# Attention and two feed-forward stages: whole q and k loads, two pairs by units, another list

## The chip, the cores and the metric

One of the eight cores of a Trainium2 chip runs the kernel. The metric is the device time of one execution in microseconds, lower being better. Before the change three runs gave 909.26, 910.92 and 911.55 us, a median of 910.92.

## What is computed

q, k and v are (4, 8, 576, 64) in f32. Attention is local: each chunk of 64 positions attends to itself alone. Its output goes through two feed-forward stages whose weights arrive as f64.

```python
scores = scale * np.matmul(q_c, k_c.transpose(0, 1, 2, 4, 3))   # per 64-position chunk
scores = scores - np.max(scores, axis=-1, keepdims=True)
attn = np.exp(scores)
attn = attn / (np.sum(attn, axis=-1, keepdims=True) + 1e-09)
x = np.matmul(attn, v_c)           # then (B*S, H*D) = (2304, 512)
y = ((x @ w_a) * (x @ w_b)) @ w_out                    # 512 -> 1536 -> 512
h = y @ w_in                                           # 512 -> 2048
out = (np.maximum(h, 0) + alpha * np.minimum(h, 0)) @ w_out2    # -> 512
```

## The kernel before

**Tiling.** The 2304 tokens are 18 units of 128 (two chunks of 64). Two units are a pair (U = 2), nine pairs in all, and attention works on a pair at a time. For the feed-forward stages units are gathered in five blocks: block 0 has two units (256 columns), blocks 1 to 4 have four (512 columns). Each f32 product is made of three f32r matmuls, of a high and a low half of either factor, so every activation and every weight is split in two.

**The list.** All of attention and the first feed-forward group are written out in START (L30 to L41) as tokens; `perform` (L504) runs them one by one. Every engine works off its own tokens strictly in that order, and waits for the data of each. A number is that of the unit, pair or weight block, or block and part.

- Lk, Lw: load q and k, and v, of a unit (sync queue, three buffers each; a load waits until the unit three before is read). `load` (L367) makes three DMAs of each: the even heads of all 128 partitions, and twice 64 partitions of the odd heads, with the halves exchanged.
- s: scores of a pair (TensorE, 64 matmuls of 64x64, L393); m, u: maximum and subtraction (VectorE, L401, L409); e: exponential (ScalarE, L417); z, r: sum and reciprocal (VectorE, L421 to L427); n: normalise (GpSimd, L431); t: four transposes of a unit (TensorE, L440); c: their copy to SBUF (ScalarE, L445); v: products with v of a pair (TensorE, 64 matmuls, L461); h, l: high half (ScalarE, L475) and low half (VectorE, L479) of x. The tiles s and px share two PSUM buffers of two banks.
- Lf: fetch of a weight block, 512 KB of f64 (sync queue, two buffers, L93). o: two passes on ScalarE (L103, L104); d: three on VectorE (L111 to L115); a: an addition on GpSimd (L125); H: high half (ScalarE, L130); W: low half (VectorE, L135). Blocks 0 to 3 are two of w_a and two of w_b, 4 and 5 are of w_out, 6 and 7 belong to the next group.
- F j.q: first products of block j, 12 matmuls (q = 0, 2 with w_a; 1, 3 with w_b); E: their way out (ScalarE copy, or VectorE product L262); h j.q, g j.q: high half (ScalarE) and low half (GpSimd, L238) of the product. B, D: second product (6 matmuls) and its way out.

F j needs h and l of all pairs in block j: F0 those of pair 0, F1 of pairs 1 and 2, F2 of 3 and 4, F3 of 5 and 6. F j.0 needs weight block 0, j.1 block 1, j.2 block 2, j.3 block 3; B needs blocks 4 and 5.

**After the list** (L531) come the first products of block 4, which read x of pairs 7 and 8, and then the groups of both stages, block by block, with one weight conversion (`job`) every fifth step. That code isn't changed.

Of the kernel before, what the change touches and what calls it, by code (L numbers as in the profile page):

```python
# [44 lines left out]
def tile_attention_moe_moe2(ctx: ExitStack, tc: tile.TileContext, qkv, w_a, w_b, w_out, w2_in, alpha, w2_out, out):  # L45
# [92 lines left out]
    WA = {}
# [46 lines left out]
        halved[0] += 1  # L185
        block_at[b] = half_high(block_at[b], jobs[b][0], jobs[b][2])

    def w_halves(b):
        m, dst, tag = jobs[b][:3]
        dst[m] = half_low(*block_at.pop(b), m, tag)  # L190

    def job(limit):

        b = halved[0]
        if b < begun[0] and jobs[b][0] < limit:
            w_high(b)
# [163 lines left out]
    with tc.manual_schedule():  # L360
# [58 lines left out]
        def at_sum(p):  # L419
            sm = ap.tile([P, U * HP, 2, 1], F32, tag="sm", name="sm")  # L420
            nc.vector.tensor_reduce(out=sm.rearrange("p h i o -> p h (i o)"), in_=prob[p], op=ALU.add, axis=AX.X)  # L421
            rec_of[p] = sm
# [6 lines left out]
        def at_norm(p):  # L429
            e = prob[p]  # L430
            nc.gpsimd.tensor_tensor(  # L431
                out=e, in0=e, in1=rec_of.pop(p).to_broadcast([P, U * HP, 2, 64]), op=ALU.mult
            )
# [14 lines left out]
        def at_pv(p):

            px = pss.tile([P, 2, HP // 2, U * P], F32, tag="s", name="px")  # L450
            for k in range(U):
                pt = pt_of.pop(U * p + k)
                t = v_t.pop(U * p + k)
                for h2 in range(HP // 2):
# [11 lines left out]
            px_of[p] = px.rearrange("p o h n -> p h o n")

        def x_part(x, c):
            return x.rearrange("p (h o) n -> p h o n", o=2)[:, :, :, c:c + U * P]

        def at_xh(p):
# [1 line left out]
            if c == 0:
                new_x(b)
            nc.scalar.activation(out=x_part(xh[b], c), in_=px_of[p], func=ACTF.Copy)  # L475

        def at_xl(p):
            b, c = block_of[p]
            nc.vector.tensor_tensor(  # L479
                out=x_part(xl[b], c), in0=px_of.pop(p), in1=x_part(xh[b], c).bitcast(F32), op=ALU.subtract  # L480
            )
# [111 lines left out]
```

## Time and profile before

| | |
|---|---|
| span of the profiled execution | 909.1 us |
| its time | 911.02 us |
| median of three runs | 910.92 us |
| TensorE matmuls | 883.1 us busy, 97%, 5208 instructions |
| VectorE, ScalarE, GpSimd | 501.4, 287.2, 297.2 us busy |
| mean granted TensorE clock | 0.992 of full speed |
| DMA | 55.36 MB, mean 61 GB/s |
| chain that ended last | TensorE 93%, DMA 3%, sync queue 3% |

PE is TensorE's matmuls, PEld its weight loads, DVE is VectorE, ACT ScalarE, POOL GpSimd, SPq the sync engine's DMA queue. Matmuls overlap, so a row's duration is longer than the step to the next. PEclk is the clock granted to TensorE, 1.00 being 2.4 GHz and about 0.5 the lower level, 1.2 GHz. The chain of waits follows what released each piece of work back from the end. In brackets behind a row stands the idle time before it and what ended it.

### The profile page before, as it was taken

What the parts mean: (1) busy time and instruction counts of PE and PEld (TensorE: products, weight loads), DVE (VectorE), ACT (ScalarE), POOL (GpSimd) and SP (SyncE); (2) the same over time, 40 slices, a digit from 0 to 9 for tenths busy, and PEclk for the clock granted to TensorE, in tenths of its full rate; (3) what the DMA queues carried; (4) which work ended last, traced back from release to release, by engine and by line L of the source; (5) the groups of instructions that cost most, each with busy time, mean ns of one, the idle gap of its engine ahead of it and who ended that gap; (6) DMA issues with size and microseconds to landing.
All of it is one profiled execution on the core that took longest, in us unless ns stands there. A gap on an engine that the chain in (4) does not pass through costs nothing.

```text
span 909.1 us, 12839 instructions
## 1 busy us (share of the span) xinstructions
PE 883.1 (97%) x5208; PEld 742.6 (82%) x5208; DVE 501.4 (55%) x772; ACT 287.2 (32%) x499; POOL 297.2 (33%) x243
## 2 busy tenths in 40 slices
PE   4789999999999999999999999999999999999998
PEld 3678888888888888888888888888888888888886
DVE  3678543443454444444353453777767676768554
ACT  2456445331422332232243353312222231223010
POOL 1333333321322222232155632333333233324131
PEclk9899999999999999999999999999999999999999
DMA  8795412210110111011010011111102010200013
GB/s 195 180 233 138 116 47 70 66 51 24 47 62 31 47 47 47 24 48 56 14 63 32 1 47 47 46 47 34 59 26 69 24 47 24 70 24 23 1 70 139
DMA packets 59242, 55.36 MB, mean 61 GB/s; under 512 B 5168, under 2 KB 53296, under 8 KB 59184
## 3 DMA queue, kind: packets, MB, share of 16 engines
q1 hardware_dynamic: 59184, 54.55, 20.8%
q8 instruction: 41, 0.67, 0.3%
q14 instruction: 17, 0.14, 0.0%
HBM read 49.82 MB, written 4.72 MB: 60 GB/s over the span
## 4 chain that ended last, share of the span: by engine, by line
PE 93%; DMA 3%; SPq 3%; ACT 1%; DVE 1%; issue 0%; ACTq 0%
PE po L228 38%; PE ph L228 22%; PE pb L228 15%; PE pa L228 15%; SPq L371 2%; DMA qk_t<-in_qkv 1%; DMA raw<-in_moe_w_out 1%; PE px L461 1%; SPq L368 1%; PE s L393 1%; PE pt L440 1%; SPq L93 0%; ACT t L103 0%; ACT wh L130 0%; DVE e L409 0%
## 5 line engine op out<-in xcount | busy, mean ns | idle before, releaser
L238 POOL TENSOR_TENSOR gl<-neg,gh 128x512 fp32r<-128x512 f32 (+1 forms) x80 | 94.8, 1185 | 184.7 <-ACT gh L233 179.8
L125 POOL TENSOR_TENSOR t<-t,raw 128x512 int32<-128x512 int32 x68 | 89.3, 1313 | 190.0 <-issue 87.9
L233 ACT ACTIVATE gh<-neg 128x512 fp32r<-128x512 f32 (+1 forms) x80 | 47.3, 591 | 278.3 <-DVE neg L322 270.3
L238 POOL TENSOR_TENSOR gl<-a_sb,gh 128x512 fp32r<-128x512 f32 (+1 forms) x60 | 71.2, 1186 | 184.9 <-ACT gh L233 179.4
L228 PE MATMUL ph<-xh,wh 128*128 128x512 f32 (+1 forms) x320 | 117.7, 368 | 0.0
L228 PE MATMUL ph<-xl,wh 128*128 128x512 f32 (+1 forms) x320 | 117.7, 368 | 0.0
L228 PE MATMUL ph<-xh,wl 128*128 128x512 f32 (+1 forms) x320 | 117.7, 368 | 0.0
L262 DVE TENSOR_TENSOR a_sb<-pb,a_sb 128x512 f32<-128x512 f32 (+1 forms) x60 | 38.1, 636 | 139.3 <-PE pb L228 138.5
L228 PE MATMUL po<-wh,gl 128*128 128x512 f32 x288 | 112.1, 389 | 0.0
L228 PE MATMUL po<-wl,gh 128*128 128x512 f32 x288 | 112.1, 389 | 0.0
L228 PE MATMUL po<-wh,gh 128*128 128x512 f32 x288 | 112.0, 389 | 0.0
L135 DVE TENSOR_TENSOR wl<-t,wh 128x512 fp32r<-128x512 f32 x68 | 69.8, 1028 | 72.9 <-ACT wh L130 72.9
L340 DVE TENSOR_TENSOR oacc<-po,oacc 128x512 f32<-128x512 f32 x126 | 83.5, 686 | 33.1 <-PE po L228 33.1
L319 DVE TENSOR_SCALAR neg<-ph,alpha_sb 128x512 f32<-128x512 f32 (+1 forms) x80 | 55.7, 696 | 73.5 <-PE ph L228 71.2
L228 PE MATMUL po<-gh,wl 128*128 128x512 f32 (+1 forms) x240 | 90.0, 375 | 3.2 <-DVE wl L135 3.2
L228 PE MATMUL pa<-xh,wl 128*128 128x512 f32 (+1 forms) x240 | 89.3, 372 | 2.1 <-ACT ptt_t L445 2.1
L228 PE MATMUL po<-gl,wh 128*128 128x512 f32 (+1 forms) x240 | 89.3, 372 | 0.0
L228 PE MATMUL po<-gh,wh 128*128 128x512 f32 (+1 forms) x240 | 89.2, 372 | 0.0
L228 PE MATMUL pa<-xl,wh 128*128 128x512 f32 (+1 forms) x240 | 88.9, 370 | 0.0
L228 PE MATMUL pa<-xh,wh 128*128 128x512 f32 (+1 forms) x240 | 88.9, 370 | 0.0
L228 PE MATMUL pb<-xh,wl 128*128 128x512 f32 (+1 forms) x240 | 88.7, 370 | 0.0
L228 PE MATMUL pb<-xl,wh 128*128 128x512 f32 (+1 forms) x240 | 88.3, 368 | 0.0
(53 smaller groups left out, 1498.3 us busy)
## 6 DMA issues: line engine op xcount, KB each, us to landing
raw<-in_moe_w_out SPq DMA_DIRECT2D x28, 512.0 KB, 3.5
raw<-in_moe_w_in SPq DMA_DIRECT2D x16, 512.0 KB, 3.7
raw<-in_moe_w_a SPq DMA_DIRECT2D x12, 512.0 KB, 3.7
raw<-in_moe_w_b SPq DMA_DIRECT2D x12, 512.0 KB, 3.6
qk_t<-in_qkv SPq DMA_DIRECT2D x18, 256.0 KB, 5.5
qk_t<-in_qkv SPq DMA_DIRECT2D x36, 128.0 KB, 5.1
out<-oacc SPq DMA_DIRECT2D x18, 256.0 KB, 2.0
v_t<-in_qkv SPq DMA_DIRECT2D x18, 128.0 KB, 3.7
```

The lines of the kernel that those rows point to most:

```text
L125: nc.gpsimd.tensor_tensor(out=ti, in0=ti, in1=raw[:, :, 0].bitcast(I32), op=ALU.add)
L135: nc.vector.tensor_tensor(out=wl, in0=wf, in1=wh.bitcast(F32), op=ALU.subtract)
L228: nc.tensor.matmul(out=dst, lhsT=a, rhs=b, start=(i == 0), stop=(i == len(steps) - 1))
L233: nc.scalar.activation(out=h, in_=src, func=ACTF.Copy)
L238: nc.gpsimd.tensor_tensor(out=l, in0=src, in1=h.bitcast(F32), op=ALU.subtract)
L262: nc.vector.tensor_tensor(out=a_sb, in0=G[m, j], in1=a_sb, op=ALU.mult)
L319: nc.vector.tensor_scalar(out=neg, in0=ph, scalar1=0.0, scalar2=alpha_sb[:, m:m + 1], op0=ALU.min, op1=ALU.mult)
L340: nc.vector.tensor_tensor(out=acc[j][:, t, :], in0=po, in1=acc[j][:, t, :], op=ALU.add)
L368: nc.sync.dma_start(out=t[:, 0::2, :], in_=src[:, 0::2, :])
L371: nc.sync.dma_start(out=t[64 * i:64 * i + 64, 1::2, :], in_=src[64 * o:64 * o + 64, 1::2, :])
L393: nc.tensor.matmul(out=s[q, i, k, hp, :], lhsT=t[r, 0, hp, q], rhs=t[r, 1, hp, q])
L440: nc.tensor.transpose(out=pt[:, hp, :], in_=e[:, h].rearrange("p i k -> p (i k)"), identity=ident)
```

## The change

`load_qk` fetches a unit's q and k with one DMA, in the order in which they lie in memory, and `load_v` fetches heads as two halves, the first whole and the second with exchanged partitions, in three DMAs as before. The exchange that q and k had in the load is made where the scores are written (`hp // 2 ^ i` in `at_scores`), and the indices of the transposes and of the products with v follow it; the tile e keeps the layout of the scores.

Every attention step takes an optional `k`: with it, it works on one unit of the pair, on one half of the same tiles (`part` makes a tile at its first use). Tokens ending in U ask for that: pairs 0 and 1 go unit by unit in s, m, u, e, z, r, n, v, h and l, the other pairs whole. Token V is W on GpSimd in place of VectorE; seven of the eight weight blocks of the list use V, the last one W. START is another order of the tokens, with the same matmuls in it.

```diff
-Lk0 Lk1 Lw0 Lw1 Lk2 s0 m0 Lk3 u0 Lf0 e0 Lw2 z0 s1 Lk4 r0 o0 m1 n0 Lk5 u1 t0 d0 e1 t1 c0 z1 a0 s2 c1 r1 H0 v0
-m2 n1 Lw3 h0 u2 Lw4 t3 l0 e2 t2 Lf1 c3 W0 c2 z2 F0.0 Lf2 r2 v1 E0.0 Lk6 n2 o1 h1 Lw5 d1 t4 o2 Lk7 t5 l1 a1
-c4 Lw6 c5 d2 H1 v2 Lf3 W1 s3 h2 Lk8 a2 l2 F0.1 H2 Lf4 m3 o3 F1.0 E0.1 Lk9 W2 h0.1 d3 F0.2 Lw7 o4 u3 g0.1 Lw8
...
+Lk0 Lf0 sU0 Lk1 mU0 uU0 o0 d0 Lk2 sU1 mU1 eU0 zU0 rU0 sU2 Lf1 o1 uU1 a0 nU0 Lk3 mU2 sU3 Lk4 d1 Lk5 a1 Lw0
+Lf2 uU2 Lw1 eU1 mU3 uU3 H0 eU3 zU1 t0 s2 V0 eU2 Lk6 Lk7 rU1 nU1 c0 o2 zU3 t1 c1 H1 vU0 zU2 rU2 Lw2 vU1 nU2
+hU0 rU3 m2 hU1 Lw3 t2 nU3 t3 c3 Lk8 c2 u2 lU0 s3 lU1 e2 F0.0 E0.0 vU2 V1 vU3 d2 z2 Lw4 a2 r2 H2 F0.1 Lf3 n2
+o3 m3 t5 hU2 u3 E0.1 V2 hU3 Lk9 Lw5 d3 Lk10 s4 lU2 lU3 a3 Lk11 Lw6 e3 t4 F0.2 Lk12 c5 c4 H3 m4 v2 u4 V3 F0.3
+Lf4 h0.1 g0.1 z3 h2 l2 e4 E0.2 s5 r3 z4 F1.0 r4 Lf5 n3 o4 E0.3 E1.0 Lk13 t6 m5 d4 F1.1 h0.3 Lk14 t7 n4 c6
+F1.2 E1.1 g0.3 o5 a4 u5 d5 a5 c7 e5 Lw7 t9 H4 z5 h1.1 g1.1 t8 v3 s6 H5 Lf6 F1.3 Lw8 h3 c9 r5 V4 E1.2 Lw9
+Lk15 m6 V5 n5 c8 l3 B0.0 Lw10 u6 v4 E1.3 t11 t10 s7 o6 D0.0 m7 h1.3 h4 c11 l4 g1.3 d6 e6 B0.1 z6 B1.0 B1.1
+c10 Lw11 a6 D0.1 D1.0 r6 Lf7 B0.2 o7 u7 v5 D0.2 h5 n6 D1.1 B1.2 Lw12 B0.3 d7 e7 Lk16 D0.3 B1.3 t12 D1.2 F2.2
+D1.3 z7 Lw13 r7 n7 t13 c12 l5 F2.0 F2.3 Lw14 c13 v6 E2.2 E2.3 E2.0 t15 F2.1 t14 h6 l6 E2.1 F3.0 Lw15 Lk17
+h2.3 h2.1 g2.3 c15 s8 Lw16 g2.1 B2.0 m8 H6 a7 c14 D2.0 E3.0 v7 F3.1 B2.1 E3.1 u8 F3.2 B2.2 h3.1 F3.3 h7 l7
+Lf8 e8 z8 H7 Lf9 D2.1 r8 E3.2 Lw17 n8 D2.2 E3.3 g3.1 V6 t17 t16 B2.3 c16 c17 v8 h8 h3.3 g3.3 l8 D2.3 W7
...
-    def half_low(wf, wh, m, tag):
+    def half_low(wf, wh, m, tag, eng):
         wl = wps[m % 4].tile([P, 512], F32R, tag=tag + "l", name="wl")
-        nc.vector.tensor_tensor(out=wl, in0=wf, in1=wh.bitcast(F32), op=ALU.subtract)
+        eng.tensor_tensor(out=wl, in0=wf, in1=wh.bitcast(F32), op=ALU.subtract)
...
-        def load(t, src):
-            nc.sync.dma_start(out=t[:, 0::2, :], in_=src[:, 0::2, :])
+        def load_qk(u):
+            t = ap.tile([P, 2, HP, P], F32, tag="qk", name="qk_t", bufs=3)
+            nc.sync.dma_start(out=t.rearrange("p a h n -> p (a h n)"), in_=qkv[u, :, 0:2 * HP * P])
+            qk_t[u] = t
+
+        def load_v(u):
+            t = ap.tile([P, HP, P], F32, tag="v", name="v_t", bufs=3)
+            src = qkv[u, :, 2 * HP * P:].rearrange("p (h n) -> p h n", n=P)
+            nc.sync.dma_start(out=t[:, 0:2, :], in_=src[:, 0:2, :])
             for i in range(2):
                 o = 1 - i
-                nc.sync.dma_start(out=t[64 * i:64 * i + 64, 1::2, :], in_=src[64 * o:64 * o + 64, 1::2, :])
-
-        def load_qk(u):
-            t = ap.tile([P, 2, HP, P], F32, tag="qk", name="qk_t", bufs=3)
-            load(t.rearrange("p a h n -> p (a h) n"), qkv[u, :, 0:2 * HP * P].rearrange("p (h n) -> p h n", n=P))
-            qk_t[u] = t
-
-        def load_v(u):
-            t = ap.tile([P, HP, P], F32, tag="v", name="v_t", bufs=3)
-            load(t, qkv[u, :, 2 * HP * P:].rearrange("p (h n) -> p h n", n=P))
+                nc.sync.dma_start(out=t[64 * i:64 * i + 64, 2:4, :], in_=src[64 * o:64 * o + 64, 2:4, :])
             v_t[u] = t
 
-        def at_scores(p):
-
-            s = pss.tile([P, 2, U, HP, 64], F32, tag="s", name="s")
-            for k in range(U):
-                t = qk_t.pop(U * p + k)
+        def units(k):
+            return range(U) if k is None else range(k, k + 1)
+
+        def flat(t, k):
+
+            if k is None:
+                return t.rearrange("p i u h o k -> p (i u h o) k")
+            return t[:, :, k].rearrange("p i h o k -> p i (h o) k")
+
...
+        def wide_as(t, k):
+            return flat(t, k).to_broadcast([P, 8 * U, 64] if k is None else [P, 2, 4, 64])
+
+        def part(of, p, k, shape, pool, tag):
+            if p not in of:
+                of[p] = pool.tile(shape, F32, tag=tag, name=tag)
+            return of[p]
+
+        def at_scores(p, k=None):
+
+            s = part(s_of, p, k, [P, 2, U, 2, 2, 64], pss, "s")
+            for kk in units(k):
+                t = qk_t.pop(U * p + kk)
                 for hp in range(HP):
                     for i in range(2):
                         for c in range(2):
                             r = slice(64 * i, 64 * i + 64)
                             q = slice(64 * c, 64 * c + 64)
-                            nc.tensor.matmul(out=s[q, i, k, hp, :], lhsT=t[r, 0, hp, q], rhs=t[r, 1, hp, q])
-            s_of[p] = s.rearrange("p i u h k -> p i (u h) k")
-
-        mx_of = {}
-        rec_of = {}
-
-        def at_max(p):
-            mx = ap.tile([P, 2, U * HP, 1], F32, tag="mx", name="mx")
-            nc.vector.tensor_reduce(
-                out=mx.rearrange("p i h o -> p (i h o)"), in_=s_of[p].rearrange("p i h k -> p (i h) k"),
-                op=ALU.max, axis=AX.X,
+                            nc.tensor.matmul(
+                                out=s[q, i, kk, hp % 2, hp // 2 ^ i, :], lhsT=t[r, 0, hp, q], rhs=t[r, 1, hp, q]
+                            )
+
+        def at_max(p, k=None):
+            mx = part(mx_of, p, k, [P, 2, U, 2, 2, 1], ap, "mx")
+            nc.vector.tensor_reduce(out=flat1(mx, k), in_=flat(s_of[p], k), op=ALU.max, axis=AX.X)
+
+        def at_sub(p, k=None):
+            e = part(prob, p, k, [P, 2, U, 2, 2, 64], ap, "e")
+            nc.vector.tensor_tensor(
+                out=flat(e, k), in0=flat(s_of[p], k), in1=wide_as(mx_of[p], k), op=ALU.subtract
             )
-            mx_of[p] = mx
-
-        def at_sub(p):
-            e = ap.tile([P, U * HP, 2, 64], F32, tag="e", name="e")
-            nc.vector.tensor_tensor(
-                out=e.rearrange("p h i k -> p i h k"), in0=s_of.pop(p),
-                in1=mx_of.pop(p).to_broadcast([P, 2, U * HP, 64]), op=ALU.subtract,
-            )
-            prob[p] = e
-
-        def at_exp(p):
-            e = prob[p]
+
...
+        def at_norm(p, k=None):
+            e = flat(prob[p], k)
+            nc.gpsimd.tensor_tensor(out=e, in0=e, in1=wide_as(rec_of[p], k), op=ALU.mult)
 
         def at_t(u):
             e = prob[u // U]
-            pt = bank([P, HP, P], "pt")
-            for hp in range(HP):
-                h = u % U * HP + hp
-                nc.tensor.transpose(out=pt[:, hp, :], in_=e[:, h].rearrange("p i k -> p (i k)"), identity=ident)
+            pt = bank([P, 2, 2, P], "pt")
+            for h in range(2):
+                for i in range(2):
+                    nc.tensor.transpose(
+                        out=pt[:, h, i, :], in_=e[:, i, u % U, h].rearrange("p o k -> p (o k)"), identity=ident
+                    )
...
-                                hp, j = 2 * h2 + odd, i ^ odd
-                                r = slice(64 * i, 64 * i + 64)
+                                r = slice(64 * (o ^ i), 64 * (o ^ i) + 64)
                                 q = slice(64 * c, 64 * c + 64)
                                 nc.tensor.matmul(
-                                    out=px[64 * j:64 * j + 64, odd, h2, k * P + 64 * c:k * P + 64 * c + 64],
-                                    lhsT=t[r, hp, q],
-                                    rhs=pt[r, hp, q],
+                                    out=px[64 * i:64 * i + 64, o, h, kk * P + 64 * c:kk * P + 64 * c + 64],
+                                    lhsT=t[r, 2 * o + h, q],
+                                    rhs=pt[r, h, i, q],
                                 )
-            px_of[p] = px.rearrange("p o h n -> p h o n")
-
-        def x_part(x, c):
-            return x.rearrange("p (h o) n -> p h o n", o=2)[:, :, :, c:c + U * P]
-
-        def at_xh(p):
+
...
-            "Lf": w_fetch, "o": w_low, "d": w_bits, "a": w_add, "H": w_high, "W": w_halves,
+            "Lf": w_fetch, "o": w_low, "d": w_bits, "a": w_add, "H": w_high,
+            "W": lambda b: w_halves(b, nc.vector), "V": lambda b: w_halves(b, nc.gpsimd),
         }
 
         def perform(token):
             letters = token.rstrip("0123456789.")
             number = token[len(letters):]
+            if letters[-1] == "U":
+                by_letter[letters[:-1]](int(number) // U, int(number) % U)
+                return
```

## Rows read from the trace of the kernel before

**Rows 1.** Page, part 2: busy tenths in 40 slices of the span.
```profile
PE   4789999999999999999999999999999999999998
...
DMA  8795412210110111011010011111102010200013
```

**Rows 2.** Windows: start:end, length, then busy us (x instructions) per engine, PEclk, DMA share, GB/s.
```profile
0.00:71.05 71.05, 48.78 (x720) 41.25 (x721) 42.01 (x59) 28.39 (x46) 22.02 (x21) 0.90 0.89 197
71.05:120.65 49.60, 49.60 (x771) 40.87 (x770) 29.76 (x35) 27.47 (x42) 14.74 (x10) 1.00 0.43 113
121.00:905.00 784.00, 784.00 (x3719) 660.22 (x3717) 428.72 (x678) 231.34 (x411) 260.43 (x213) 1.00 0.14 45
...
24.80:30.00 5.20, 3.13 (x89) 2.85 (x81) 4.46 (x5) 2.99 (x4) 0.96 (x1) 1.00 0.23 63
30.00:33.00 3.00, 3.00 (x24) 2.78 (x28) 1.36 (x3) 0.13 (x1) 1.40 (x1) 0.51 0.72 164
```

**Rows 3.** Chain of waits, 0 to 200 us: start, us, engine, tile, line, count.
```profile
104.06 1.09 PE s L393 x64
...
112.98 0.87 PE pt L440 x8
...
126.09 2.72 PE pa L228 x12
...
136.97 1.43 PE pa L228 x12
```

**Rows 4.** The same chain in the front.
```profile
7.17 0.60 SPq L371
...
16.14 6.47 DMA qk_t<-in_qkv
...
43.41 6.61 DMA raw<-in_moe_w_out
```

**Rows 5.** DMA: the page's issues; queue q1 in 58:64; queue q1 in 126:140 (packets, MB, share).
```profile
raw<-in_moe_w_out SPq DMA_DIRECT2D x28, 512.0 KB, 3.5
...
q1 hardware_dynamic: 2691, 1.66, 113.0%
...
q1 hardware_dynamic: 746, 1.51, 31.2%
```

**Rows 6.** Groups of 0 to 71.1 us (busy, mean ns), then two timeline rows of VectorE.
```profile
L401 DVE TENSOR_REDUCE mx<-s 128x16 f32<-128x1024 f32 x6 | 7.3, 1219 | 14.2 <-PE s L393 14.2
...
L262 DVE TENSOR_TENSOR a_sb<-pb,a_sb 128x512 f32<-128x512 f32 x2 | 1.3, 660 | 0.1
...
L445 ACT ACTIVATE ptt_t<-pt 128x512 f32<-128x512 f32 x6 | 3.2, 585 | 0.0
...
L103 ACT ACTIVATE t<-raw 128x512 f32<-128x512 f32 x7 | 4.7, 668 | 20.6 <-DMA raw<-in_moe_w_out 7.5 <-DMA raw<-in_moe_w_a 6.4 <-DMA raw<-in_moe_w_b 4.3
...
77.36 0.17 DVE L426 TENSOR_SCALAR sm<-sm 128x16 f32<-128x16 f32 x1
77.56 0.25 DVE L427 RECIPROCAL sm<-sm 128x16 f32<-128x16 f32 x1
```

**Rows 7.** Timeline of VectorE and GpSimd: start, us, engine, line, operation.
```profile
51.26 0.43 DVE L112 TENSOR_SCALAR t<-t 128x512 uint32<-128x512 uint32 x1
51.72 0.69 DVE L115 SCALAR_TENSOR_TENSOR t<-raw,t 128x512 uint32<-128x512 uint32 x1
...
70.01 2.02 DVE L112 TENSOR_SCALAR t<-t 128x512 uint32<-128x512 uint32 x1
...
68.10 1.28 POOL L238 TENSOR_TENSOR gl<-a_sb,gh 128x512 fp32r<-128x512 f32 x1
69.84 1.90 POOL L431 TENSOR_TENSOR e<-e,sm 128x1024 f32<-128x1024 f32 x1 [0.46 <-DMA qk_t<-in_qkv]
```

**Rows 8.** Timeline of ScalarE and VectorE at the end of START.
```profile
117.77 1.03 ACT L475 ACTIVATE xh<-px 128x1024 fp32r<-128x1024 f32 x1 [0.46 <-PE px L461]
...
118.82 1.23 DVE L479 TENSOR_TENSOR xl<-px,xh 128x1024 fp32r<-128x1024 f32 x1 [5.04 <-ACT xh L475]
```

More of the change, by code (lines that the diff above doesn't have):

```diff
@@ L186, in w_high, with w_halves @@
         block_at[b] = half_high(block_at[b], jobs[b][0], jobs[b][2])
-    def w_halves(b):
+    def w_halves(b, eng):
         m, dst, tag = jobs[b][:3]
-        dst[m] = half_low(*block_at.pop(b), m, tag)
+        dst[m] = half_low(*block_at.pop(b), m, tag, eng)
     def job(limit):
@@ L196, in job @@
             w_high(b)
-            w_halves(b)
+            w_halves(b, nc.vector)
         b = begun[0]
@@ L351, in tile_attention_moe_moe2 @@
     s_of = {}
+    mx_of = {}
     prob = {}
+    rec_of = {}
     pt_of = {}
@@ L365, in tile_attention_moe_moe2 @@
         make_identity(nc, ident)
-        def load(t, src):
-            nc.sync.dma_start(out=t[:, 0::2, :], in_=src[:, 0::2, :])
-            for i in range(2):
-                o = 1 - i
-                nc.sync.dma_start(out=t[64 * i:64 * i + 64, 1::2, :], in_=src[64 * o:64 * o + 64, 1::2, :])
         def load_qk(u):
             t = ap.tile([P, 2, HP, P], F32, tag="qk", name="qk_t", bufs=3)
-            load(t.rearrange("p a h n -> p (a h) n"), qkv[u, :, 0:2 * HP * P].rearrange("p (h n) -> p h n", n=P))
+            nc.sync.dma_start(out=t.rearrange("p a h n -> p (a h n)"), in_=qkv[u, :, 0:2 * HP * P])
             qk_t[u] = t
@@ L379, in load_v, with flat1 @@
             t = ap.tile([P, HP, P], F32, tag="v", name="v_t", bufs=3)
-            load(t, qkv[u, :, 2 * HP * P:].rearrange("p (h n) -> p h n", n=P))
-            v_t[u] = t
-        def at_scores(p):
-            s = pss.tile([P, 2, U, HP, 64], F32, tag="s", name="s")
-            for k in range(U):
-                t = qk_t.pop(U * p + k)
+            src = qkv[u, :, 2 * HP * P:].rearrange("p (h n) -> p h n", n=P)
+            nc.sync.dma_start(out=t[:, 0:2, :], in_=src[:, 0:2, :])
+            for i in range(2):
+                o = 1 - i
+                nc.sync.dma_start(out=t[64 * i:64 * i + 64, 2:4, :], in_=src[64 * o:64 * o + 64, 2:4, :])
+            v_t[u] = t
+        def units(k):
[4 more added lines that the diff above has]
+            return t[:, :, k].rearrange("p i h o k -> p i (h o) k")
+        def flat1(t, k):
+            if k is None:
+                return t.rearrange("p i u h o k -> p (i u h o k)")
+            return t[:, :, k].rearrange("p i h o k -> p i (h o k)")
+        def wide_as(t, k):
[8 more added lines that the diff above has]
+                t = qk_t.pop(U * p + kk)
                 for hp in range(HP):
@@ L407, in at_sub @@
-        def at_sub(p):
-            e = ap.tile([P, U * HP, 2, 64], F32, tag="e", name="e")
-            nc.vector.tensor_tensor(
-                out=e.rearrange("p h i k -> p i h k"), in0=s_of.pop(p),
-                in1=mx_of.pop(p).to_broadcast([P, 2, U * HP, 64]), op=ALU.subtract,
-            )
-            prob[p] = e
-        def at_exp(p):
-            e = prob[p]
-            nc.scalar.activation(out=e, in_=e, func=ACTF.Exp, scale=SCALE)
[L419 to L422, printed above, removed]
@@ L426, in at_rec, with at_exp, at_sum @@
+        def at_exp(p, k=None):
+            e = flat(prob[p], k)
+            nc.scalar.activation(out=e, in_=e, func=ACTF.Exp, scale=SCALE)
+        def at_sum(p, k=None):
+            sm = part(rec_of, p, k, [P, 2, U, 2, 2, 1], ap, "sm")
+            nc.vector.tensor_reduce(out=flat1(sm, k), in_=flat(prob[p], k), op=ALU.add, axis=AX.X)
+        def at_rec(p, k=None):
+            sm = flat1(rec_of[p], k)
             nc.vector.tensor_scalar(out=sm, in0=sm, scalar1=1e-9, scalar2=None, op0=ALU.add)
@@ L427, in at_rec @@
             nc.vector.reciprocal(out=sm, in_=sm)
[L429 to L433, printed above, removed]
+        def at_norm(p, k=None):
+            e = flat(prob[p], k)
+            nc.gpsimd.tensor_tensor(out=e, in0=e, in1=wide_as(rec_of[p], k), op=ALU.mult)
         def at_t(u):
             e = prob[u // U]
-            pt = bank([P, HP, P], "pt")
-            for hp in range(HP):
-                h = u % U * HP + hp
-                nc.tensor.transpose(out=pt[:, hp, :], in_=e[:, h].rearrange("p i k -> p (i k)"), identity=ident)
+            pt = bank([P, 2, 2, P], "pt")
+            for h in range(2):
+                for i in range(2):
+                    nc.tensor.transpose(
+                        out=pt[:, h, i, :], in_=e[:, i, u % U, h].rearrange("p o k -> p (o k)"), identity=ident
+                    )
@@ L441, in at_t, with at_pv @@
             pt_of[u] = pt
         def at_copy(u):
-            t = gp.tile([P, HP, P], F32, tag="a", name="ptt_t", bufs=3)
+            t = gp.tile([P, 2, 2, P], F32, tag="a", name="ptt_t", bufs=3)
             nc.scalar.activation(out=t, in_=pt_of[u], func=ACTF.Copy)
             pt_of[u] = t
[L448 to L454, printed above, removed]
+        def at_pv(p, k=None):
+            px = part(px_of, p, k, [P, 2, 2, U * P], pss, "s")
+            for kk in units(k):
+                pt = pt_of.pop(U * p + kk)
+                t = v_t.pop(U * p + kk)
+                for h in range(2):
@@ L455, in at_pv @@
                     for c in range(2):
-                        for odd in range(2):
+                        for o in range(2):
                             for i in range(2):
-                                hp, j = 2 * h2 + odd, i ^ odd
-                                r = slice(64 * i, 64 * i + 64)
+                                r = slice(64 * (o ^ i), 64 * (o ^ i) + 64)
                                 q = slice(64 * c, 64 * c + 64)
                                 nc.tensor.matmul(
-                                    out=px[64 * j:64 * j + 64, odd, h2, k * P + 64 * c:k * P + 64 * c + 64],
-                                    lhsT=t[r, hp, q],
-                                    rhs=pt[r, hp, q],
-                                )
@@ L466, in at_pv, with x_parts @@
[L466 to L471 removed]
+                                    out=px[64 * i:64 * i + 64, o, h, kk * P + 64 * c:kk * P + 64 * c + 64],
+                                    lhsT=t[r, 2 * o + h, q],
+                                    rhs=pt[r, h, i, q],
+                                )
+        def x_parts(p, k):
             b, c = block_of[p]
[L473 to L475 removed]
@@ L477, in at_xl, with at_xh @@
[L477 to L481, printed above, removed]
+            n = U * P
+            px = px_of[p].rearrange("p o h n -> p (o h) n")
+            if k is not None:
+                c, n = c + k * P, P
+                px = px[:, :, k * P:k * P + P]
+            return b, slice(c, c + n), px
+        def at_xh(p, k=None):
+            b, s, px = x_parts(p, k)
+            if s.start == 0:
+                new_x(b)
+            nc.scalar.activation(out=xh[b][:, :, s], in_=px, func=ACTF.Copy)
@@ L483, in tile_attention_moe_moe2, with at_xl @@
+        def at_xl(p, k=None):
+            b, s, px = x_parts(p, k)
+            nc.vector.tensor_tensor(out=xl[b][:, :, s], in0=px, in1=xh[b][:, :, s].bitcast(F32), op=ALU.subtract)
         order = []
```

9 lines of the change are left out of this document (removed).

## Prediction, made before the changed kernel was run

> **What bounds the kernel now.** I read the tenths of the span first [rows 1]: from the third slice on TensorE is at nine tenths or more, and only the first two slices and a dip in the fourth lie open, while the DMA engines are at seven to nine tenths in the first three and at two or less later. The windows [rows 2] give the sizes. From 121 to 905 us TensorE is busy for all 784.00 us at full clock; the change issues the same operations in the same order there, so nothing is to be had. From 71.05 to 120.65 it is busy for 49.60 of 49.60 us. Before 71.05 it is busy for 48.78 us, idle for 22.27. So the question is when TensorE comes to the end of START, which is at 120.65 us now.
>
> Busy is not the measure of the front, since small matmuls stand there waiting for data, and at half clock. I take the work at full speed from the chain of waits [rows 3]: a pair's scores 1.09 us, its products with v, as many of the same size, the same, its transposes 0.87; an F, 12 matmuls, 1.43 at 256 columns and 2.72 at 512; a B, 6 of them, half of that, 0.72 and 1.36. START holds 9 x (1.09 + 1.09 + 0.87) = 27.5, F0 4 x 1.43 = 5.7, F1 to F3 12 x 2.72 = 32.6, B0 2.9, B1 and B2 8 x 1.36 = 10.9: 79.6 us. So 120.65 - 79.6 = **41.0 us are lost in START before**. Up to the start of t6 at 71.05 the list has 6 scores, 6 transposed units, 3 products, F0, F1 and B0, 31.9 us, so 39.2 of the loss lie there; 1.9 are small steps later. The changed list has the same matmuls: what it must lower is the 41.0.
>
> Where the chain runs in the front [rows 4]: sync-queue issues one after another (0.60 us each, 16 us nearly without a break), then DMA legs of 6.47 us for q and k and 6.61 for a weight block, with one more alike between them. So loading sets the pace, by issues and by bytes in flight.
>
> **The loads.** A unit's q and k were three DMAs, now one; v stays at three. 18 x 2 issues of some 0.60 us go, 21.6 us of sync-queue time [rows 4], about ten of them ahead of the first F. Bytes stay. What stays open is the rate with long runs. While mostly 512-byte runs of q and k were in flight, 1.66 MB in 6 us, 276 GB/s at a share of 113% [rows 5]; weight blocks alone, runs of 1 and 4 KB as the new loads have, 1.51 MB at 31.2% of 14 us, which is 346 GB/s at a share of 1, and 390 at 1.13. I take 330, between, since v is left with shorter runs and 64-partition halves; ends 276 and 390.
>
> The Trainium skill, "DMA: Bandwidth & Descriptors", Specifications, speaks against a gain here: it gives 512 B as the smallest transfer at line rate, and q and k had just that. The two shares above differ from it (245 against 346 GB/s at a share of 1), though no row shows long q and k runs. By that page only the issues would be saved.
>
> A weight block alone lands 3.5 us after its issue [rows 5], so Lk0, issued at 0.7, lands at 4.3 to 4.4 and a later load at 4.4 + 3.18 us for each MiB behind it in the list: Lk3 (3 MiB with it) 12.4, Lf2 17.9, Lk7 21.9, Lf3 27.5, Lk9 29.0. The sync queue's issues and its waits for free buffers (Lk3 behind sU0, Lf2 behind a0) come earlier than these.
>
> **One unit at a time.** VectorE before the first F has, by the groups and rows of [rows 6], per pair max, subtract and sum, 1.22 each (one of three alike stands there), and 0.45 for the reciprocal (0.17 + 0.25 and a step). Half-size operations it never shows on these lines; nearest is 128x512 from PSUM at 0.66. Bounds 0.61 (half) and 1.22 (no saving); I take 0.66. Scalar copies of 128x512 are 0.59. VectorE's list to lU1 is then four units of 3 x 0.66 + 0.45 = 9.7, d0 and d1 2 x 1.55 (0.43 twice and 0.69 with the steps [rows 7]) = 3.1, m2 and u2 2.4, lU0 and lU1 1.3: 16.5 us from 5.6 (Lk0 4.4, sU0 1.2 at low clock): 22.1. Beside it, two chains end as late: Lf2 17.9, o2 2 x 0.67 (which stands ahead of c1 on ScalarE), c1 0.59, then H1, hU0, hU1 1.8 (vU1 beside them) and lU1 0.66: 22.3; and Lk7 21.9 plus half of s3, 22.5. **F0.0 starts at 22.6**, against 29.96 now.
>
> **From F0.0 on**, step by step. F0.0, vU2, vU3, F0.1: to 26.5. VectorE d2 24.0, z2 and r2 25.6; GpSimd n2 1.90: 27.5; t5 28.0. The second half of s4 on Lk9: 29.6; t4 and F0.2: 31.5. ScalarE has o3 on Lf3 to 28.9, hU2, hU3 30.1, e3 31.1, c5, c4 32.3; v2: 33.4. The fourth weight block: o3 28.9, d3 30.4, a3 31.8, H3 behind c4 32.9, V3 1.30: 34.2. F0.3 to 35.6, s5 36.7. VectorE up to l2 (d3 30.4, lU2, lU3, m4, u4, z3, l2) 36.6. F1.0, t6, F1.1, t7, F1.2 follow without a gap: **45.7**. At full speed this is 6 scores 6.5, 8 units 3.5, 3 products 3.3, F0 5.7, three F1 8.2 = 27.2, so **18.5 us are lost**. Behind it I find no wait: B0 is ready (E1.1 43.3, then e5, H4 and h1.1 46.6, g1.1, V4 and V5 3 x 1.30: 50.5; TensorE is there at 51.5, behind t9, t8, v3, s6, F1.3), and VectorE has some 23 us of list left for over 50 of TensorE.
>
> **Halves of weights to GpSimd.** Seven subtractions of 0.69, as L115's of the same size [rows 7], leave VectorE and seven of 1.30 (nearest, 128x512 subtract into gl [rows 7]) join GpSimd. Up to g0.3 GpSimd then has about 22 us in 35, so it hides them, except V3 above, where 0.6 is in the chain. VectorE and GpSimd also stop each other: L112 took 2.02 us, not 0.43, while n ran from 69.84 [rows 7]. One such wait in the chain, part covered: 0.7 (0 to 1.6 each).
>
> **The end of the list.** Before, v8 was followed by F3.3, 2.95 us, under which xh 1.03 and xl 1.23 ended at 120.05 [rows 8]. Now v8 is TensorE's last entry; what comes next is block 4's first product, which reads both. TensorE waits 1.03 + 1.23 + steps = 2.3. An idle of 2.07 us (5.20 - 3.13) was followed by 3.00 us at 0.51 of the clock, the lower level [rows 2], 1.5 lost; so 3.8 in all (2.3 if the clock stays, 4.6 if the wait counts twice).
>
> **The new indices** of scores, transposes and products keep 64, 8 and 64 matmuls per pair of the same shapes, and the subtract's output runs of 64 become whole rows: I take nothing (under 0.1 us on 1.22).
>
> **Sum.** 79.6 + 18.5 + 1.9 = 100.0; end of list 3.8; some 25 steps between engines at 0.06, 1.5, and the lock 0.7: 106.0. Before 120.65: 14.6 us gained. The profiled execution took 911.02 us for a span of 909.1; its time is 0.1 over the median of 910.92. **911.0 - 14.6 = 896.4 us.**
>
> **Rivals.**
> - Rate unchanged (the skill's page above would give it too): at 258 GB/s, between 245 and 276, a MiB takes 4.06 us, Lf3 lands at 33.9, 6.4 later, and v2, F0.3 and l2 with it: gain 8, **903**. For it: at 113% the engines were full [rows 5]. Against: the two rates at share 1.
> - Units not independent: the two units of a pair share one s, px and e tile, and if their operations wait for each other as if whole, or half-size operations cost as full ones, VectorE's list before F0.0 grows by ten times 0.56 = 5.6: gain 9, **902**.
> - Better: rate 390, no clock loss, half-size at 0.61: Lk9 at 25.7, gain 20, **891**.
> - Slower: GpSimd's one queue. a, V and n now stand in line, and V is ahead of n2, n3 and of g1. If its operations stretch beyond 35/22 = 1.6 times (L112's 2.02 for 0.43 is the widest stretch shown), t5, F0.2, v2, F0.3, F1.0 and B0 each wait about 2 us and the clock falls each time: 2.07 + 1.5 = 3.6 each, six times 21 us, so a gain of 14.6 becomes a loss of 7: **918**. It decides at V3, the first place where that queue is in my chain. For it: the 2.02 for L112. Against: GpSimd is busy 22.02 of 71.05 us now.
>
> **Chances.** Forecast (893 to 900) 0.48; better 0.15; rate or units (900 to 907) 0.25; within 0.3% of the time before, 2.7 us, which is about what can be told from no change, 0.05; slower 0.07. Faster 0.88. The range takes in the bounds of rate, half-size cost and end stall: 888 to 905.
>
> **What would show it.** q and k as single DMAs landing some 3.5 us after issue when alone; F0.0 near 22.6 us; F1.2 ending near 46; a wait of about 2.3 us for xl between v8 and block 4's first product, near 105 us, with a lower clock behind it; TensorE full from there. I am wrong if F0.0 starts after 27, if TensorE idles over 3 us between F0.0 and the end of F1.3, or if DMA rates in the first 30 us stay under 280 GB/s.

## The result, and the profile after

The changed kernel takes 897.33 us (median of 4 runs, 896.42 to 897.70), against 910.42 (909.26 to 911.55, 4 runs): a ratio of 0.9855, interval 0.9838 to 0.9872, 13.1 us less. The prediction was 896.4. The profiled execution took 897.7 us for a span of 895.8.

The tenths of the page, answering [rows 1]:

```profile
PE   5899899999999999999999999999999999999998
...
DMA  8853122110110120111010020111111010200013
```

The DMA engines are as busy as before in the first two slices, but the loads of the list end earlier: the third and fourth slices stand at five and three tenths, before at nine and five. The windows, in the columns of [rows 2], cut at the first F (22.97), the end of F1.2 (50.70), of v8 (104.84), and where block 4 begins (107.19):

```profile
0.00:22.97 22.97, 13.21 (x337) 11.17 (x337) 15.23 (x31) 11.36 (x20) 9.90 (x14) 1.00 0.88 299
22.97:50.70 27.73, 24.17 (x358) 21.16 (x359) 22.70 (x34) 14.64 (x26) 13.69 (x10) 0.88 0.69 232
50.70:104.84 54.14, 53.94 (x797) 44.97 (x794) 26.70 (x35) 27.74 (x47) 21.55 (x15) 1.00 0.41 117
104.84:107.19 2.35, 0.00 (x0) 0.00 (x0) 1.28 (x2) 2.03 (x3) 0.71 (x1) 1.00 0.03 7
107.19:891.70 784.51, 784.51 (x3719) 660.65 (x3720) 429.62 (x678) 230.22 (x410) 259.17 (x213) 1.00 0.13 45
...
32.20:40.20 8.00, 7.99 (x128) 7.45 (x128) 6.13 (x8) 5.16 (x9) 3.26 (x3) 0.62 0.88 306
```

From 107.19 on TensorE is full, and the rest of the span is as long as before (788.6 us; before, 909.1 - 120.65 = 788.5): all of the gain lies in START, whose end moved from 120.65 to 107.19, 13.5 us. Of the 107.19 us 79.6 are work [rows 3], so 27.6 are lost and not 41.0. Where, the chain of waits shows (start, us, engine, tile, line, count; as [rows 3, 4]). In it pa and pb are first products (F), po second ones (B), pt transposes, s at L416 scores and s at L474 products with v, whose tile px has the tag s too:

```profile
0.73 3.77 DMA qk_t<-in_qkv
...
4.55 1.18 PE s L416 x32
...
22.97 1.70 PE pa L229 x12
...
24.68 7.48 DMA qk_t<-in_qkv
...
32.21 1.13 PE s L416 x32
33.34 1.04 PE pt L452 x4
34.39 2.56 PE pa L229 x12
...
50.70 0.88 PE pt L452 x8
...
103.70 1.14 PE s L474 x64
...
104.86 1.03 ACT xh L493
...
105.91 1.24 DVE xl L497
...
107.19 3.02 PE pa L229 x12
```

The sync queue, which filled the chain's first 16 us in [rows 4], isn't in this one. Besides Lk0 one load is, Lk9, issued at 24.68 and landed 7.48 us later. TensorE waited 2.56 us for it, and ScalarE 4.34 us for the fourth weight block, Lf3 (rows of both engines):

```profile
30.93 0.66 ACT L104 ACTIVATE t<-raw 128x512 f32<-128x512 f32 x1 [4.34 <-DMA raw<-in_moe_w_b]
...
32.21 1.13 PE L416 MATMUL s<-qk_t 64*64 64x64 f32 x32 [2.56 <-DMA qk_t<-in_qkv]
```

Behind the wait for Lk9 TensorE runs at a lower clock: 0.62 on the mean from 32.2 to 40.2, an F of 256 columns in 2.56 us and not 1.43. At the end stands the foreseen wait of 2.4 us for xl. This is one profile of the kernel; a second one (x12_again, below) loses its time in other places.

### The profile page after: what moved, and what is told of

Its sections match the earlier page's. It is cut to its first block, busy times and chain, and to the rows that moved or that the text cites. A ratio compares the mean times of both kernels' runs of the same rounds, so it can differ in the third digit from the quotient of the medians.

```text
span 895.8 us, 12808 instructions
## 1 busy us (share of the span) xinstructions
PE 876.3 (98%) x5208; PEld 738.0 (82%) x5208; DVE 496.2 (55%) x777; ACT 286.0 (32%) x503; POOL 305.0 (34%) x252
## 3 DMA queue, kind: packets, MB, share of 16 engines
q1 hardware_dynamic: 37872, 54.54, 18.4%
## 4 chain that ended last, share of the span: by engine, by line
PE 97%; DVE 1%; DMA 1%; POOL 0%; ACT 0%; issue 0%
PE po L229 38%; PE ph L229 22%; PE pa L229 17%; PE pb L229 16%; DMA qk_t<-in_qkv 1%; PE s L474 1%; PE pt L452 1%; PE s L416 1%; DVE e L426 0%; DVE mx L422 0%; DVE t L116 0%; DVE xl L497 0%; DVE sm L436 0%; POOL e L445 0%; ACT xh L493 0%; DVE t L113 0%
## 5 line engine op out<-in xcount | busy, mean ns | idle before, releaser
L239 POOL TENSOR_TENSOR gl<-a_sb,gh 128x512 fp32r<-128x512 f32 (+1 forms) x60 | 71.1, 1185 | 180.4 <-ACT gh L234 179.9
L136 DVE TENSOR_TENSOR wl<-t,wh 128x512 fp32r<-128x512 f32 x61 | 64.4, 1055 | 70.5 <-ACT wh L131 70.5
L229 PE MATMUL pb<-xh,wh 128*128 128x512 f32 (+1 forms) x240 | 88.3, 368 | 0.0
```

What stands on the lines that cost most here:

```text
L136: eng.tensor_tensor(out=wl, in0=wf, in1=wh.bitcast(F32), op=ALU.subtract)
L229: nc.tensor.matmul(out=dst, lhsT=a, rhs=b, start=(i == 0), stop=(i == len(steps) - 1))
L239: nc.gpsimd.tensor_tensor(out=l, in0=src, in1=h.bitcast(F32), op=ALU.subtract)
```

## The experiments

Twelve more were run, eleven new kernels and the changed one again, in three groups (x1 to x4, x5 to x8, x9 to x12), each group beside runs of its own of the kernel before. Ratios are to those and are what is compared; the time in the last column is the ratio times 910.42. The changed kernel's two ratios differ by 0.0016, or 1.4 us; differences of that size between groups tell nothing.

| kernel | median | ratio | interval | on 910.42 |
|---|---|---|---|---|
| changed | 897.33 | 0.9855 | 0.9838 to 0.9872 | 897.2 |
| x1_old_list | 898.07 | 0.9853 | 0.9838 to 0.9869 | 897.0 |
| x2_three_loads | 908.12 | 0.9959 | 0.9947 to 0.9972 | 906.7 |
| x3_pairs | 899.95 | 0.9866 | 0.9854 to 0.9879 | 898.2 |
| x4_no_V | 899.74 | 0.9867 | 0.9854 to 0.9880 | 898.3 |
| x5_short_runs | 901.49 | 0.9884 | 0.9867 to 0.9900 | 899.9 |
| x6_Lk9_early | 896.88 | 0.9837 | 0.9822 to 0.9851 | 895.6 |
| x7_end_cover | 896.79 | 0.9840 | 0.9824 to 0.9856 | 895.9 |
| x8_both | 895.40 | 0.9822 | 0.9807 to 0.9836 | 894.2 |
| x9_psum_late | 893.22 | 0.9799 | 0.9785 to 0.9813 | 892.1 |
| x10_v8_early | 893.73 | 0.9803 | 0.9790 to 0.9817 | 892.5 |
| x11_best | 892.46 | 0.9790 | 0.9774 to 0.9805 | 891.3 |
| x12_again (the changed one) | 897.70 | 0.9839 | 0.9823 to 0.9855 | 895.8 |

**Loads or order?** First the changed code with the list of before:

```diff
-Lk0 Lf0 sU0 Lk1 mU0 uU0 o0 d0 ...
+Lk0 Lk1 Lw0 Lw1 Lk2 s0 m0 Lk3 ...
```

> The changed code with START of before: whole q and k loads and the new layouts, but no unit tokens, no V and the old order. Theory (the front is paced by loading, so loads and order both count): the 21.6 us of sync-queue time that go bring F0.0 from 29.96 to about 25 and the weight blocks forward, but the old order still puts Lf0 behind six loads and lets B0 wait for its weights: 904 us, 902 to 907. Rival (the order and the units make all of it): within 2 us of 910.4. Rival (the loads make all of it): 897 to 899.

Measured: 0.9853, the whole gain; my 904 was wrong and the rival right that gives the loads everything (with them here come v's load in halves and the new indices). Its windows up to its first F, to 63 and to the end of its list:

```profile
0.00:23.07 23.07, 11.26 (x273) 9.78 (x273) 14.07 (x18) 9.16 (x12) 5.79 (x9) 1.00 0.67 212
23.07:63.00 39.93, 35.41 (x545) 30.90 (x546) 31.62 (x45) 23.56 (x41) 18.52 (x13) 0.96 0.75 240
63.00:107.26 44.26, 43.00 (x674) 34.99 (x673) 24.73 (x32) 23.24 (x36) 13.28 (x8) 1.00 0.43 117
```

The old list comes to its first F at 23.07 us, where the new one is at 22.97, and ends at 107.26, where the new one ends at 107.19. The first F is not quite the same point in both: the old list has one pair's scores fewer ahead of it (273 matmuls with the first of F, the new list 337), and its second F starts at 34.60, where the new list's starts at 25.67. It makes most of that up by the end of the list, where the new list's last products end 2.4 us earlier, at 104.84, and then TensorE waits. Then the reverse, the new list with the old number of loads:

```diff
-            nc.sync.dma_start(out=t.rearrange("p a h n -> p (a h n)"), in_=...)
+            nc.sync.dma_start(out=d[:, 0::2, :], in_=src[:, 0::2, :])
+            for i in range(2):
+                nc.sync.dma_start(out=d[64*i:64*i+64, 1::2, :], in_=src[64*i:64*i+64, 1::2, :])
```

> The changed kernel, with q and k of a unit fetched in three DMAs of 512-byte runs again (even heads of 128 partitions, odd heads of twice 64), without the exchange. Theory: every Lk takes two more issues, 1.2 us, ten of them before the last load that F1 needs, and short runs lower the rate, so F0.0 comes some 6 us later, near 29, and the time is 903 to 907. Rival (only the new order counts): within 2 us of 897.3.

Measured: 0.9959, 906.7, as the theory had it; the first F starts at 32.06. So with slow loads the new list is worth 0.4% (3.7 us), with whole loads nothing that can be told (-0.2 us by the changed kernel's first ratio, 1.2 by its second), and the loads are worth 13.4 us under the old list and 9.5 under the new (10.9 by the second ratio).

**Issues or runs?** One DMA, but runs of 512 bytes:

```diff
-            t = ap.tile([P, 2, HP, P], F32, tag="qk", name="qk_t", bufs=3)
+            t = ap.tile([P, 2, HP, P + 4], F32, tag="qk", name="qk_t", bufs=3)
```

> The changed kernel with one DMA for q and k as before it, but into a tile whose head rows are padded by 16 bytes, so that it moves in runs of 512 bytes. It parts the number of issues from the length of runs. Theory (long runs are faster): DMA rates between 10 and 20 us fall from 352 GB/s to about 280, Lk9 lands 2 to 4 us later, time 899 to 902. Rival (512 bytes are as good, only the issues counted): within 1 us of 897.3. The Trainium skill, DMA: Bandwidth & Descriptors, Specifications, gives 512 B as enough for line rate and so stands on the rival's side.

Measured: 0.9884, 899.9. The queue's rows for 10 to 20 us, of the changed kernel, of x5 and of x2 (packets, MB, and share, which is the packets' time as a part of the time of 16 engines, so it passes 100% where packets overlap):

```profile
q1 hardware_dynamic: 1924, 3.50, 101.1%
```

```profile
q1 hardware_dynamic: 4664, 2.93, 112.7%
```

```profile
q1 hardware_dynamic: 4119, 2.35, 119.3%
```

At a higher share the short runs move less: 2.93 MB in 10 us at 112.7% is 260 GB/s at a share of 1, against 346. The Trainium skill ("DMA: Bandwidth & Descriptors", Specifications) gives 512 B as the smallest transfer at line rate. These rows don't bear it out, and here the measurement decides.

From x5 to the changed kernel, where only the runs grow, 2.6 us are won (4.1 by x12_again; the interval of x5 is clear of the second one, not of the first). From x2 to x5, where one DMA stands for three at the same run length, it is 6.8 us. That this is the time of the two issues isn't shown: x2's queue issues nearly without a break, but in these ten us its DMA engines don't stand idle for it: they are at 119.3% and move still less, 197 GB/s at a share of 1. The three DMAs differ from the one also in form, two of them covering 64 partitions, and no run parts the form from the issues.

**Units and V.** Pairs 0 and 1 whole, and all low halves on VectorE:

```diff
-... sU0 Lk1 mU0 uU0 ... sU1 mU1 eU0 zU0 rU0 ...
+... Lk1 ... s0 m0 ... u0 ... e0 ...
```

> The changed kernel with pairs 0 and 1 whole: each pair's token stands where the token of its second unit stood, and t0 and t2 behind n0 and n1, since they read the whole pair's normalised e. Theory: the softmax of unit 0 waits for unit 1's load and VectorE idles from 5.7 to about 8.5, while the list is as long, less a few short operations; F0.0 comes 2 to 4 us later and the time is 900 to 902. Rival (loading is the bound and units give nothing): 896 to 898.5.

```diff
-            ... "V": lambda b: w_halves(b, nc.gpsimd),
+            ... "V": lambda b: w_halves(b, nc.vector),
```

> The changed kernel with V on VectorE, that is all low halves of weights there as before. Theory: V0 adds 0.69 us to VectorE ahead of lU1, V1 to V3 come while it has idle time, and GpSimd is relieved of 1.3 us each: 897 to 899, no difference that can be told. Rival (VectorE is the bound in all of the front): 7 x 0.69 = 4.8 us longer, 901 to 902.

Measured: 0.9866 and 0.9867, 1.0 and 1.1 us above the changed kernel by its first ratio, 2.5 by its second; the intervals overlap the first's and touch the second's, so either is worth a little at most. x3's time is that of its rival, x4's that of its theory. x3's first F starts at 25.01, inside what the changed kernel itself shows (22.90 in one profile, 25.63 in the other), so the 2 to 4 us that the units were to bring there aren't shown. In x4 a product with w_b waits 1.9 us for a low half on VectorE; in the changed kernel's first profile none waits for one, in its second one waits 0.6 us, on GpSimd:

```profile
PE pb L229 <- DVE wl L136: 1.9, 1, 1.9
```

**The wait for Lk9.** The sync queue of the changed kernel at 19 to 26 us (start, us, line, tile):

```profile
19.44 0.33 SPq L378 DMA_DIRECT2D v_t<-in_qkv  x1
19.82 1.87 SPq L381 DMA_DIRECT2D v_t<-in_qkv  x2
21.74 0.58 SPq L372 DMA_DIRECT2D qk_t<-in_qkv  x1
22.42 0.38 SPq L378 DMA_DIRECT2D v_t<-in_qkv  x1
22.84 1.11 SPq L381 DMA_DIRECT2D v_t<-in_qkv  x2
24.05 0.53 SPq L94 DMA_DIRECT2D raw<-in_moe_w_b  x1
24.68 0.45 SPq L372 DMA_DIRECT2D qk_t<-in_qkv  x1
```

Lw3 stands at its head until vU0 has read its buffer, at 19.4; Lk8, Lw4, Lf3 and Lk9 queue behind it. So Lk8, Lf3 and Lk9 were moved ahead:

```diff
-rU2 Lw2 vU1 ... c3 Lk8 c2 ... s3 lU1 ... F0.1 Lf3 n2 ... hU3 Lk9 Lw5
+rU2 Lk8 Lf3 Lw2 vU1 ... c3 c2 ... s3 Lk9 lU1 ... F0.1 n2 ... hU3 Lw5
```

> The changed kernel with Lk8 and Lf3 moved ahead of Lw2 and Lk9 to right behind s3, so that they don't stand in the sync queue behind Lw3, which waits for vU0 until 19.4. Theory: the DMA engines' gap at 20 to 23 us closes, Lk9 lands near 27 and not at 32.16, the 2.56 us wait in s4 goes and with it the half clock of 30 to 40 us: 4 us less, 892 to 895. Rival (another wait takes its place, the weight block's chain or VectorE, so the wait just moves): 896 to 898.

Measured: 0.9837, above the 892 to 895 expected, below the changed kernel's first ratio but not its second: by time alone unclear. The trace says more. Windows of the changed kernel at 20 to 23 us, and of x6 there and at 30 to 40:

```profile
20.00:23.00 3.00, 3.00 (x97) 2.65 (x89) 1.60 (x4) 2.17 (x5) 1.24 (x1) 1.00 0.50 142
```

```profile
20.00:23.00 3.00, 3.00 (x52) 2.55 (x51) 1.48 (x4) 1.62 (x4) 1.21 (x1) 1.00 1.05 366
...
30.00:40.00 10.00, 9.07 (x226) 8.11 (x217) 9.70 (x15) 4.34 (x7) 5.18 (x4) 1.00 0.94 320
```

The DMA engines' gap closed (share 0.50 to 1.05), the clock stayed at 1.00 and the chain reached block 4 at 104.14, three us earlier. But then, in the chain of x6:

```profile
102.87 1.24 DVE xl L497
...
104.14 4.61 PE pa L229 x12
```

The same 12 matmuls took 4.61 us, where they took 3.02 in the changed kernel's first profile and take 2.72 at full speed: half of what this front won over that one went into the clock behind the wait at the end. It isn't x6's doing, as the second profile of the changed kernel shows below: 4.37 us there.

**The wait at the end.** Block 3's second products, which read no x, ahead of block 4's first ones:

```diff
-        for i, (f, args) in enumerate(order[NB - 1][2] + order[NB - 2][3]):
+        for i, (f, args) in enumerate(order[NB - 2][3] + order[NB - 1][2]):
```

> The changed kernel with the end of the list covered: h3.3 and g3.3 ahead of v8, and behind the list the second products of block 3 ahead of block 4's first products. Theory: the 2.40 us wait for xl between v8 and block 4's first product goes, with 0.3 of low clock: 2.7 us less, 894 to 895.5. Rival (block 3's second products wait for g3.3 instead): within 1 us of 897.3.

> The changes of x6_Lk9_early and x7_end_cover together. Theory: the two lie far apart, so the gains add: 889 to 892.5. Rival (the time won in the front is lost again before the end of the list): as x7_end_cover alone, 894 to 896.

Measured: x7 0.9840, span 895.4 beside 895.8; x8 0.9822. Both theories missed, and the chain of x7 shows why:

```profile
103.30 1.14 PE s L474 x64
...
105.52 1.24 DVE xl L497
...
106.80 5.74 PE po L229 x24
```

A product that reads no x still waits for xl. What it shares with xl is PSUM, TensorE's output memory: behind the list a second pool of tiles, ps1, takes the banks of px, and xl of pair 8 reads px last. So ps1 was taken four products later, and, as a second way, v8 was put ahead of B2.3 and F3.3 with nothing changed behind the list:

```diff
+            if i == 4:
+                pps.append(ctx.enter_context(tc.tile_pool(name="ps1", bufs=4, space=PSUM)))
```

> x7_end_cover, with the second PSUM pool taken only after the four second products of block 3. In x7 the wait for xl of 2.4 us stayed, though those products read no x. Theory: the wait is for PSUM, since the pool ps1 takes the banks of px, which xh and xl of pair 8 still read; with ps1 taken four products later TensorE doesn't wait: 2.4 us less than x7 and than the changed kernel, 893 to 895 by the ratio. Rival (the wait is for x after all, or for g3.3): as x12_again.

```diff
-... B2.2 h3.1 F3.3 h7 l7 ... t17 t16 B2.3 c16 c17 v8 h8 h3.3 g3.3 l8 D2.3 W7
+... t17 t16 Lw17 c16 c17 B2.2 v8 D2.2 h8 B2.3 l8 F3.3 D2.3 E3.3 h3.3 V6 W7 g3.3
```

> The changed kernel with the softmax of pair 8 (u8, e8, z8, r8, n8) and t17, t16, c16, c17, v8, h8, l8 moved ahead, so that v8 stands before B2.3 and F3.3, as before the change it stood before F3.3. Nothing behind the list is changed. Theory: 4.1 us of matmuls cover xh and xl, whichever of x and PSUM the wait was for: 2.4 us less than x12_again, 893 to 895. Rival (u8 ahead of E3.1 holds up another product): within 1 us of x12_again.

> The changed kernel itself once more, as the reference for the three beside it: 895.8 us of span and a ratio of 0.9855 again, between 0.984 and 0.987.

> x9_psum_late with the earlier Lk8, Lf3 and Lk9 of x6_Lk9_early. Theory: 3 us from the front and 2.4 or more from the end of the list: 890 to 892.5 by the ratio (0.977 to 0.980). Rival (x6 and x8 had the whole of it, the clock gives the rest back): 893 to 895.

Measured: x9 0.9799 and x10 0.9803 beside 0.9839 for the changed kernel (a little under what was expected of it), 3.7 and 3.3 us less, where 2.4 was expected; x11 0.9790, 4.5 less (892.46 against 897.70 in the same group, 5.2), as expected. x9's end of list, and then that of x12_again:

```profile
102.88 1.09 PE s L474 x64
103.97 5.67 PE po L229 x24
109.64 2.72 PE pa L229 x12
```

```profile
104.39 1.24 DVE xl L497
...
105.67 4.37 PE pa L229 x12
```

In x9 TensorE goes on without a gap. x7, whose products need only the banks, waited; x9, which needs neither, doesn't. In x12_again the low clock (0.65 granted) took 4.37 - 2.72 = 1.65 us more. x11, faster than both kernels, is the version to keep.

**One kernel, several profiles.** x7, x9, x10 and x12_again have the changed kernel's list up to F1.2 and far beyond it, x6, x8 and x11 the one with the early loads. From their traces, in us (the first column by the first matmul's own row, which is 22.90 where the chain has 22.97):

| profile | first F starts | F1.2 ends | TensorE goes on behind the list |
|---|---|---|---|
| changed | 22.90 | 50.70 | 107.19 |
| x12_again | 25.63 | 48.95 | 105.67 |
| x7 | 24.28 | 49.72 | 106.80 |
| x9 | 25.38 | 49.12 | 103.97 |
| x10 | 25.70 | 48.14 | 103.51 |
| x6, early loads | 23.71 | 47.06 | 104.14 |
| x8, early loads | 24.64 | 47.24 | 104.06 |
| x11, early loads | 24.20 | 46.83 | 100.93 |

In x12_again TensorE waits 2.60 us for c1 (ScalarE's copy) early on and runs at the lower clock there, the wait for Lk9 is 0.96, and the clock is 1.00 from 30 to 40 us; only Lf3 is as late as in the first profile:

```profile
22.00:26.00 4.00, 4.00 (x87) 3.48 (x80) 2.47 (x5) 2.87 (x5) 0.97 (x1) 0.61 0.65 184
```

```profile
21.15 1.13 PE L474 MATMUL s<-ptt_t,v_t 64*64 64x64 f32 x32 [2.60 <-ACT ptt_t L459]
...
30.73 0.69 ACT L104 ACTIVATE t<-raw 128x512 f32<-128x512 f32 x1 [2.41 <-DMA raw<-in_moe_w_b]
32.36 0.69 PE L416 MATMUL s<-qk_t 64*64 64x64 f32 x32 [0.96 <-DMA qk_t<-in_qkv]
```

So how long TensorE waits for Lk9, and whether the clock falls behind it, changes from profile to profile (2.19 us in x7, 1.31 in x9, no wait in x10). What holds in all eight is that F1.2 ends at 48.1 to 50.7 with the late loads and at 46.8 to 47.2 with the early ones. Which of the three moved loads does it isn't parted; by the times the move is worth 0.8 us from x9 to x11 and 1.7 from x7 to x8, and the intervals of either pair overlap.

## Why the prediction was right, and where it was not

- **Where the time is.** That START alone could move held: 788.6 us lie behind it, 788.5 before. So did how much is lost in it: 27.6 with 0.3 more in the clock behind the end, where the sum had 26.4.
- **The loads.** Right, and larger in its share than I had it. Lk0 landed 3.77 us after its issue (3.6 to 3.7 said); the rate was 352 GB/s in 10 to 20 us (330 taken). The first rival, an unchanged rate, fell.
- **One unit at a time.** F0.0 started at 22.97 (22.6 said), but that is luck: with the same list it started at 24.28 to 25.70 in four other profiles, at the latest 3.1 us behind the forecast. In x12_again it waits behind the very chain that was named, Lf2, o2 and c1, with Lf2's block taken up at 19.40 for 17.9. What the step was to bring isn't shown either: x3, with whole pairs, starts its first F at 25.01, and given whole loads the old list with its whole pairs takes as long. The list and the units, on which half of the working rests, are worth nothing beyond the loads as long as the end of the list stands as it does. The half-size operations cost what was taken, in these groups of 0 to 60 us 685, 677 and 665 ns for 660, so the second rival fell too:

```profile
L422 DVE TENSOR_REDUCE mx<-s 128x8 f32<-128x512 f32 x4 | 2.7, 685 | 5.8 <-PE s L416 5.8
L426 DVE TENSOR_TENSOR e<-s,mx 128x512 f32<-128x512 f32 x4 | 2.7, 677 | 0.1
L436 DVE TENSOR_REDUCE sm<-e 128x8 f32<-128x512 f32 x4 | 2.6, 665 | 0.0
L136 POOL TENSOR_TENSOR wl<-t,wh 128x512 fp32r<-128x512 f32 x6 | 7.7, 1284 | 1.1 <-ACT wh L131 1.1
```

- **From F0.0 on** is the step that failed in size: F1.2 ended at 50.70 and not 45.7, and at 48.14 to 49.72 in the four other profiles of this list. In the first profile 7.7 us are lost between F0.0 and the end of F1.2 (27.73 less 20.0 of work), not 3.1; in x12_again 3.3 are lost there, but 18.4 ahead of F0.0 for 15.4. "The sync queue's issues and its waits for free buffers ... come earlier than these" was wrong at Lf3 and Lk9, which stand behind Lw3's wait: Lf3's block was taken up at 30.93 for 27.5 (30.73 in x12_again), and Lk9 landed at 32.16 for 29.0. The 2.56 us of waiting for Lk9 were followed by 8 us at a clock of 0.62, some 3.0 lost, and I had counted the lower clock at the end of the list only. That the place of these loads is a cause, the early ends of F1.2 in x6, x8 and x11 show. One of my signs of being wrong came up here: TensorE idles for 3.56 us between F0.0 and the end of F1.3 (33.58 less 30.02 busy), over the 3 that I had named (1.66 in x12_again).
- **V on GpSimd** took 1.284 us each (1.30 said). It is hidden in the first profile; in x12_again F0.3 waits 0.6 us for V3, just as said. The slower rival didn't come up.
- **The end of the list.** The wait came as said, 2.35 us, but its reason was incomplete: TensorE waits for px's banks as well as for x (x7 against x9). The low clock behind it cost 0.3 us in this profile and 1.65 and 1.9 in those of x12_again and x6, for 1.5 said.
- **The 2.2 us for steps between engines and for the lock** (VectorE and GpSimd holding each other up) can't be read off as a row: the loss of 1.7 from 50.70 to 104.84 is 0.2 under its term, and 0.4 lies ahead of F0.0. So the gain came within 1.5 us (13.1 for 14.6) because that reserve, 2.2, and what the end's clock didn't take, 1.2, covered 3.4 of the 4.6 that the front lost. That the terms cancel so well is luck; the mechanism that makes the gain, the loads, is not.

Why the new list shows no gain over the old is settled for its end: with the wait cured (x10) it is 0.0050, 4.5 us, below x1_old_list, whose list never had that wait, since F3.3 stands behind v8 there. That comparison is between groups, which can be 1.4 us apart for one kernel; by the traces block 4 begins at 103.51 in x10 and at 107.26 in x1, 3.75 us apart.

## What to carry to other kernels

Where loading sets the pace, count the DMAs and not only the bytes: one DMA for three was worth 6.8 us here, longer runs 2.6 to 4.1, and a new order of some 300 operations up to 4.5, once its last wait was cured. Check a written-out order at its seam: cover the last evacuation, and ask which memory the next stage takes, not only which data it reads. A wait of 2.4 to 2.6 us on TensorE cost its own length in these profiles and between 0.1 and 3.0 us more in clock. And before you name one wait as the cause, look at a second profile of the same kernel: here the wait for Lk9 was 2.56 us in one and 0.96 in the other.

## What was not expected of the hardware

After waits of the same 2.4 us at the same place, the same 12 matmuls took 3.02, 4.37 and 4.61 us in three profiles (changed, x12_again, x6), with 1.00, 0.65 and 0.63 of the clock granted. In x7 and x8 the same wait was followed by 24 matmuls in 5.74 and 5.73 us, hardly more than the 5.67 of x9, which has no wait there. Whether the clock falls to its lower level there differs from run to run or with what ran before, and these runs don't settle which.
